# Warm-up of 5 large and 65 small matmuls for 90 small ones, and batch 1's factors split one pair ahead

## The chip, the cores and the metric

The kernel runs on one core of a Trainium2 chip. The core has five engines, each with its own instruction stream: TensorE (PE, matmuls and weight loads), VectorE (DVE), ScalarE (ACT), GpSimd (POOL) and SyncE (SP, which here only issues transfers). The metric is the device time of one execution in microseconds. An engine works its stream in order and waits at an instruction whose semaphores have not arrived. Line numbers (L657) are those of the kernel file.

## What is computed

Chunked attention with a memory, over 4 batches of 768 tokens and 8 heads of 64, and behind it a mixer: a low-rank mixing of tokens and a two-layer network.

```python
for c in range(nc):                       # chunks of 32 queries, 24 of them
    q_c = q[:, :, c_start:c_end]
    k_ctx = k[:, :, l_start:r_end]        # 16 keys to the left, 8 to the right
    k_full = np.concatenate([mem_k, k_ctx], axis=2)
    v_full = np.concatenate([mem_v, v_ctx], axis=2)
    a = softmax(scale * q_c @ k_full.T)   # written out in the reference
    out[:, :, c_start:c_end] = np.matmul(a, v_full)

h = xt @ U @ V                            # xt is x with tokens last
u = x + h.transpose(0, 2, 1)
ch = np.maximum(u @ w_ch1, 0.0) @ w_ch2   # 512 -> 2048 -> 512
return (u + ch).astype(np.float32)
```

The weights U, V, w_ch1 and w_ch2 arrive as 64-bit floating-point words, the rest as 32-bit ones.

## The kernel before

Work goes batch by batch. While the mixer of batch b runs on PE, the attention of batch b + 1 is woven into it, a step at a time. The hidden layer is cut into 16 slices of 128 (f), the 768 tokens into two blocks of 384.

**The front (0 to about 58 us).** Batch 0's attention runs alone. `keep_clock(n, m)` (L144) sets aside n large and m small matmuls on a tile of zeros (`busy`); the next `att_ps` (L135) issues them into the bank that it hands out: large ones 128x512 (L138), small ones 32x64 (L140). Each is a weight load and a matmul, two PE instructions. The first call, `keep_clock(0, START)` (L818) with START = 90 (L30), stands ahead of the first transposes (`turn`, L583).

**Batch 0's mixer (about 57 to 230 us), `both_blocks` (L1187).** For each slice f, `w1_step` (L1119) multiplies by the first weights; ACT makes the rounded hidden values `hh` (L1125), DVE the rest `hl` (L1126); `w2_step` (L1173, L1178) multiplies by the second weights. In the same stage the 64-bit weights are decoded: ACT takes the two halves of the words (L217, L231), DVE joins them (L224, L225, L238), ACT casts the high part (L392, into `w1h`, a `w` pair or `w2last`) and DVE takes the low part (L368). Batch 1's attention is woven in by `place`: key transposes (`turn`, L583, copied by ACT in L601 to L613 into `kall`), query transposes (copied in L643 into `qt`, four copies for a pair of banks), scores (`s_turn`, L657, 128 small matmuls), weights turned (`t_part`, L742), the product with the values (`av_turn`, L760, 128 small matmuls). Transposes, scores and value products of the attention take their banks from one pool of three (`ps_a`), in turn; a bank is free again when what reads it has been read.

**Batches 1 to 3, `fast`.** A pair of slices is worked out with seven products in place of eight (`products`, L1399). The factors of the products are sums of weight blocks, made by GpSimd for batch 1 (`prepare`, L1293) and loaded for batches 2 and 3; `build_factor` splits each into a cast (ACT, L1367, tiles `w1l` for factors 0 to 3 and `s` for 4 to 6) and a rest (DVE, L1368). Some of a pair's factors are split while the pair before it is multiplied. `fold_both` (L1310) turns x of the next batch and forms the folded tokens `th` and `tl`; `put_by` (L1097) notes x tiles for storing, and `let_go` (L1101) issues the stores on ACT (L1104) at the next border.

**What sets the order.** SP's, PE's and GpSimd's streams are in the order of the code. DVE's is so until L1208, ACT's until L1204; from there a scheduler with a simulated timeline orders them by priority. ACT's order in batch 0's mixer (from the third step on) therefore depends on that timeline, the warm-up included, though no code of that stage is touched.

PE's instructions come from memory by a queue of its own (queue 8 in the profile), 16 KB a packet.

Of the kernel before, what the change touches and what calls it, by code (L numbers as in the profile page):

```python
# [26 lines left out]
PACED = {ET.DVE}  # L27
HEAD = {ET.Activation}
FIRST = 3000
START = 90  # L30
FILL = [2, 2, 0, 0, 0, 0]
BANKS = (
    "o0 o1 h h a a a h h a a o0 o1 a a h h o0 o1 a a h h o0 o1 a a o0 o1 a h h a a o0 a a"
# [22 lines left out]
def chunk_attn_then_mixer_kernel(  # L56
# [13 lines left out]
    nc = tc.nc  # L70
# [18 lines left out]
    TB = 3  # L89
# [54 lines left out]
    def keep_clock(n, m=0):  # L144
        warm[0] += n
        small[0] += m
# [23 lines left out]
    for j in range(4):  # L170
        nc.gpsimd.tensor_copy(
            out=rep[32 * j:32 * j + 32],
            in_=ident[32 * j:32 * j + 32, None, 32 * j:32 * j + 32].broadcast_to([32, 3, 32]),
# [252 lines left out]
    def attention(b, xs):  # L426
# [367 lines left out]
        if b == 0:  # L794
# [20 lines left out]
            load_consts()  # L815
            regroup(kraw, kn, "kn", 0)
            regroup(qraw, qn, "qn", 0)
            keep_clock(0, START)  # L818
            k0 = []
            for h in two:  # L820
                k0.append(turn(kn.pop((0, h))))
# [217 lines left out]
    xs = {}  # L1039
# [58 lines left out]
    def put_by(b, t):  # L1098
        held.append((x_d[b, t], xs.pop((b, t))))
# [210 lines left out]
    def fold_both(b):  # L1310
        th, tl = turned[0]
        for tt in range(TB):
            sl = slice(tt * P, (tt + 1) * P)
            with tc.high_priority(offset=HIGH):
                psv = []
                for t in (tt, TB + tt):
                    ps = att_ps()
                    psv.append(ps.rearrange("c (a n) -> c a n", a=NCK))
                    for c in range(NCK):
                        nc.tensor.transpose(out=psv[-1][:, c, :], in_=xs[b, t][:, c * P:(c + 1) * P], identity=ident)  # L1320
                b1, b2 = psv
                f32 = [slot([P, 2, 2, P], F32, "fold") for _ in range(4)]
                base = f32[0]
                nc.scalar.copy(out=base[:, 0], in_=b1[:, 0:2, :])
                nc.scalar.copy(out=base[:, 1], in_=b2[:, 2:4, :])
                for i, ps, c, j, op in (
                    (2, b1, 2, 0, ALU.subtract), (4, b1, 2, 1, ALU.add), (0, b2, 2, 0, ALU.add),
                    (3, b2, 0, 0, ALU.add), (1, b2, 0, 1, ALU.subtract),
                ):
                    nc.vector.tensor_tensor(  # L1330
                        out=f32[1 + i // 2][:, i % 2], in0=ps[:, c:c + 2, :], in1=base[:, j], op=op,
                    )
                for n, (i, m) in enumerate(((5, 2), (0, 2), (2, 2), (4, 1))):
                    nc.scalar.copy(out=th[:, i:i + m, :, sl], in_=f32[n][:, 0:m])
                    nc.vector.tensor_tensor(  # L1335
                        out=tl[:, i:i + m, :, sl], in0=f32[n][:, 0:m], in1=th[:, i:i + m, :, sl].bitcast(F32),
                        op=ALU.subtract,
                    )
            for t in (tt, TB + tt):
                put_by(b, t)  # L1340
            yield

    fast_pools = []
# [15 lines left out]
    factors = {}  # L1359

    def build_factor(p, n):
        if n < WLO:
            s = wlo.tile([P, NCK, P], F32R, name="w1l")
        else:
            s = fast_pools[0].tile([P, NCK, P], F32R, name="s", bufs=len(PRODUCTS) - WLO)
        total = mixed.pop((p, n))
        nc.scalar.copy(out=s[:, 0:2], in_=total)  # L1367
        nc.vector.tensor_tensor(out=s[:, 2:4], in0=total, in1=s[:, 0:2].bitcast(F32), op=ALU.subtract)  # L1368
        factors[p, n] = s
# [10 lines left out]
    def seven(b, kept, last):  # L1380

        th, tl = turned[0]
        ta, tb = fast_pools[1]
        made = {}

        def products(p):
            banks = [ps_h.tile([P, 512], F32, name="ps_h"), ps_a.tile([P, 512], F32, name="ps_a")]
            banks.append(ps_h.tile([P, 512], F32, name="ps_h"))
            banks = [bank_[:, :TOK] for bank_ in banks]
            b1, b2, b3 = banks  # L1390
            kept[2 * p], kept[2 * p + 1] = (
                fast_pools[0].tile([P, TOK], F32, name="kept", bufs=NF // 2) for _ in range(2)
            )
            hid_ = {}
            for n, (i, at_) in enumerate(PRODUCTS):
                s = factors.pop((p, n))
                parts = [(s, c, t, c) for c in range(2) for t in (th, tl)] + [(s, 2 + c, th, c) for c in range(2)]
                for m, (w, wc, t, c) in enumerate(parts):
                    nc.tensor.matmul(  # L1399
                        out=banks[at_], lhsT=w[:, wc, :], rhs=t[:, i, c, :], start=(n < 3 and m == 0),  # L1400
                        stop=(m + 1 == len(parts)), skip_group_check=True,
                    )
                with tc.high_priority(offset=HIGH):
                    if n == 0:
                        nc.scalar.copy(out=ta, in_=b1)  # L1405
                    elif n == 1:
                        nc.vector.tensor_tensor(out=ta, in0=b2, in1=ta, op=ALU.subtract)
                    elif n == 2:
                        nc.vector.tensor_tensor(out=tb, in0=b3, in1=ta, op=ALU.add)  # L1409
                    elif n == 3:  # L1410
                        nc.scalar.copy(out=kept[2 * p], in_=b1)
                    elif n == 4:
                        hid_[1] = split_hidden(b2)
                        nc.vector.tensor_tensor(out=tb, in0=tb, in1=b2, op=ALU.subtract)
                    elif n == 5:
                        nc.vector.tensor_tensor(out=ta, in0=b3, in1=ta, op=ALU.add)  # L1416
                    else:
                        nc.vector.tensor_tensor(out=kept[2 * p + 1], in0=b1, in1=tb, op=ALU.add)
                        hid_[0] = split_hidden(ta)
                    for m in ((5,), (6,), (), (), (), (), ())[n]:  # L1420
                        build_factor(p, m)
                    if p + 1 < NF // 2 or not last:
                        for m in ((), (), (0,), (1, 2), (), (3,), (4,))[n]:
                            build_factor((p + 1) % (NF // 2), m)
                if n in (2, 6):
                    fast_border()
            made[p] = hid_

        def first_block(p):
            hid_ = made.pop(p)  # L1430
            for side in (1, 0):
                f = 2 * p + side
                ends = True if p == NF // 2 - 1 and side == 0 else None
                w2_step(b, 0, f, 0, p == 0 and side == 1, ends, *hid_[side])
                fast_border()

        def second_block(fs, ends, each):
            for f in fs:
                hid_ = split_hidden(kept.pop(f))
                w2_step(b, 1, f, 2, f == fs[0], ends if f == fs[-1] else None, *hid_)  # L1440
                each()

        return products, first_block, second_block
# [90 lines left out]
```

## Time and profile before

| | us |
|---|---|
| median of three runs | 658.36 (656.92 to 664.51) |
| the profiled execution | 658.64 |
| its span, first to last instruction | 656.8 |
| PE busy | 625.0 (95%) |
| DVE busy | 420.6 (64%) |
| ACT busy | 306.1 (47%) |
| GpSimd busy | 77.9 (12%) |

The span is a little shorter than the time, since the time includes what lies around the program. Mean granted PE clock: 0.995 of full speed. A timeline row gives start, duration from the first start to the last end, engine, line, operation, tiles, how many instructions stand in the row and, in brackets, the idle time ahead of it with what ended it; matmuls overlap, so durations of neighbouring rows do too. "issue" means that nothing the profile shows was waited for.

### The profile page before, as it was taken

How to read it: one execution, taken by the hardware profiler on the slowest of the kernel's cores; microseconds unless marked ns; L12 is line 12 of the kernel's file. 1: busy time of each engine (PE TensorE's matmuls, PEld its weight loads, DVE VectorE, ACT ScalarE, POOL GpSimd, SP SyncE). 2: the span in 40 equal slices, each digit the busy share in tenths (PEclk: the TensorE clock that was granted, in tenths of full speed). 3: DMA queues.
4: the chain of work that ended last, by engine and by line, in shares of the span. 5: the costliest groups of instructions: out<-in, count | busy, mean ns of one | idle time of the engine just before them, and what ended most of it. 6: DMA issues, size and time to landing. Idle time of an engine off the chain costs nothing.

```text
span 656.8 us, 15763 instructions
## 1 busy us (share of the span) xinstructions
PE 625.0 (95%) x6196; PEld 547.3 (83%) x6198; DVE 420.6 (64%) x887; ACT 306.1 (47%) x772; POOL 77.9 (12%) x136
## 2 busy tenths in 40 slices
PE   7788999998899898899999999999999999999997
PEld 6567999987778797788788899988979899989986
DVE  4976997886428855556866965645756965427442
ACT  4666676684214445533333646533533643315321
POOL 3700011100021343324400000000000000000000
PEclk9998999999989999999999999999999999999999
DMA  8997684775514659233532489333522673101012
GB/s 208 192 333 255 222 257 156 208 210 143 147 66 160 190 147 241 89 99 130 165 135 83 126 214 222 94 87 112 167 77 83 214 227 97 49 11 38 1 69 76
DMA packets 132724, 95.25 MB, mean 145 GB/s; under 512 B 88746, under 2 KB 109994, under 8 KB 132650
## 3 DMA queue, kind: packets, MB, share of 16 engines
q1 hardware_dynamic: 123130, 72.87, 39.8%
q10 hardware_dynamic: 6480, 11.80, 4.7%
q0 software_dynamic: 3040, 9.57, 3.7%
q8 instruction: 49, 0.80, 0.5%
q14 instruction: 25, 0.20, 0.1%
HBM read 68.65 MB, written 24.64 MB: 142 GB/s over the span
## 4 chain that ended last, share of the span: by engine, by line
PE 79%; DVE 7%; DMA 5%; issue 3%; ACT 3%; SPq 2%; POOL 0%; DVEq 0%; ACTq 0%; POOLq 0%
PE ps_h L1399 18%; PE acc L1173 13%; PE ps_a L1399 7%; PE ps_h L1119 7%; PE acc L1178 6%; PE ps_h L1173 6%; PE ps_a L1173 4%; PE ps_h L1178 3%; PE ps_a L583 2%; PE ps_a L1178 2%; PE ps_a L760 2%; PE ps_a L657 2%; PE ps_h L1165 1%; PE ps_a L742 1%; PE ps_a L1320 1%
## 5 line engine op out<-in xcount | busy, mean ns | idle before, releaser
L1173 PE MATMUL acc<-w,hh 128*128 128x512 f32 x366 | 97.5, 401 | 1.0 <-DVE w L368 1.0
L1399 PE MATMUL ps_h<-th,w1l 128*128 128x384 f32 x288 | 83.4, 343 | 5.1 <-ACT w1l L1367 2.3
L1173 PEld LDWEIGHTS acc<-w,hh 128*128 128x128 f32 x366 | 66.9, 188 | 15.3 <-issue 1.5
L1399 PEld LDWEIGHTS ps_h<-th,w1l 128*128 128x128 f32 x288 | 52.7, 188 | 9.6 <-DVE part L1416 2.9
L1375 DVE SCALAR_TENSOR_TENSOR hl<-kept,hh 128x384 fp32r<-128x384 f32 x48 | 26.7, 557 | 49.0 <-PE ps_a L1178 22.4
L1374 ACT ACTIVATE hh<-kept 128x384 fp32r<-128x384 f32 x48 | 25.4, 530 | 62.2 <-PE ps_a L1173 38.1
L1399 PE MATMUL ps_h<-th,s 128*128 128x384 f32 x192 | 53.0, 337 | 0.2 <-DVE part L1409 0.2
L1178 PE MATMUL acc<-w,hl 128*128 128x512 f32 x183 | 52.3, 394 | 0.0
L1399 PE MATMUL ps_h<-tl,w1l 128*128 128x384 f32 x144 | 48.5, 337 | 0.5 <-DVE tl L1335 0.5
L1173 PE MATMUL ps_h<-w,hh 128*128 128x512 f32 x156 | 43.0, 397 | 0.0
L1119 PE MATMUL ps_h<-uh,w1h 128*128 128x384 f32 x124 | 42.4, 348 | 0.0
L1119 PE MATMUL ps_h<-ul,w1h 128*128 128x384 f32 x124 | 41.2, 340 | 0.0
L1178 PEld LDWEIGHTS acc<-w,hl 128*128 128x128 f32 x183 | 34.8, 190 | 7.6
L1293 POOL TENSOR_TENSOR sums<-val 128x256 f32<-128x256 f32 x40 | 29.9, 762 | 92.3 <-DMA val<-vald 90.0
L1173 PE MATMUL ps_a<-w,hh 128*128 128x512 f32 x132 | 38.3, 394 | 1.7 <-ACT hh L1125 1.7
L1405 ACT COPY part<-ps_h 128x384 f32<-128x384 f32 x24 | 11.5, 480 | 58.8 <-PE ps_h L1399 36.8
L1399 PEld LDWEIGHTS ps_h<-th,s 128*128 128x128 f32 x192 | 35.1, 187 | 0.5 <-issue 0.5
L1367 ACT CAST s<-sums 128x256 fp32r<-128x256 f32 x72 | 28.4, 405 | 14.5 <-PE ps_h L1399 14.4
L1368 DVE TENSOR_TENSOR s<-sums,s 128x256 fp32r<-128x256 f32 x72 | 29.5, 418 | 6.0 <-ACT s L1367 6.0
L1368 DVE TENSOR_TENSOR w1l<-sums,w1l 128x256 fp32r<-128x256 f32 x48 | 24.8, 517 | 13.0 <-ACT w1l L1367 11.7
L1173 PEld LDWEIGHTS ps_h<-w,hh 128*128 128x128 f32 x156 | 28.4, 188 | 5.6
L1125 ACT ACTIVATE hh<-ps_h 128x384 fp32r<-128x384 f32 x31 | 15.1, 490 | 36.9 <-PE ps_h L1119 36.8
(279 smaller groups left out, 1412.5 us busy)
## 6 DMA issues: line engine op xcount, KB each, us to landing
sums<-sumsd SPq DMA_DIRECT2D x32, 256.0 KB
rw<-in_moe_w_ch_dram SPq DMA_DIRECT2D x14, 512.0 KB
xd<-x ACTq DMA_DIRECT2D x27, 256.0 KB
x<-xd SPq DMA_DIRECT2D x27, 256.0 KB
vb<-in_v_dram SPq DMA_DIRECT2D x56, 98.0 KB
raw<-in_moe_w_ch_dram SPq DMA_DIRECT2D x20, 256.0 KB
qn<-in_q_dram SPq DMA_DIRECT2D x36, 128.0 KB
out_dram<-x ACTq DMA_DIRECT2D x18, 256.0 KB
```

Of the source, the lines that this page charges most:

```text
L583: nc.tensor.transpose(out=psv[:, p, r, :], in_=half[:, r, 2 * p:2 * p + 2, :].rearrange("n h d -> n (h d)"), identity=ident,)
L657: nc.tensor.matmul(out=psv[s][CK * i:CK * i + CK, t, p % 2, p // 2, :], lhsT=qt[p // 2][rows, p % 2, NI * t + i, :], rhs=kall[rows, NB * ( ...
L1119: nc.tensor.matmul(out=ph[:, :TOK], lhsT=w[:, c, :], rhs=u[c], start=(m == 0), stop=(m + 1 == len(parts)),)
L1125: nc.scalar.activation(out=hh, in_=ph[:, :TOK], func=AF.Relu)
L1173: nc.tensor.matmul(out=acc[tt], lhsT=h[:, sl], rhs=w, start=(begins and m == 0), stop=False,)
L1178: nc.tensor.matmul(out=acc[tt], lhsT=hl[:, sl], rhs=w2h[f], start=False, stop=ends is not None)
L1293: nc.gpsimd.tensor_tensor(out=two[:, m % 2], in0=a, in1=b_, op=getattr(ALU, op))
L1367: nc.scalar.copy(out=s[:, 0:2], in_=total)
L1368: nc.vector.tensor_tensor(out=s[:, 2:4], in0=total, in1=s[:, 0:2].bitcast(F32), op=ALU.subtract)
L1374: nc.scalar.activation(out=hh, in_=src, func=AF.Relu)
L1375: nc.vector.scalar_tensor_tensor(out=hl, in0=src, scalar=0.0, in1=hh.bitcast(F32), op0=ALU.max, op1=ALU.subtract,)
L1399: nc.tensor.matmul(out=banks[at_], lhsT=w[:, wc, :], rhs=t[:, i, c, :], start=(n < 3 and m == 0), stop=(m + 1 == len(parts)), skip_group_c ...
```

## The change

Three edits. START becomes a pair, 5 large and 65 small matmuls, 140 PE instructions for 180. `fold_both` issues the store of each x tile itself, within the high-priority block, where it had noted it with `put_by`. In `products`, factors 5 and 6 are split in their own pair only where they have not been yet; in batch 1 factors 3 and 4 of the next pair are split after product 5, and 5 and 6 after product 6.

```diff
--- before.py
+++ after.py
@@ -27,7 +27,7 @@
 PACED = {ET.DVE}
 HEAD = {ET.Activation}
 FIRST = 3000
-START = 90
+START = 5, 65
 FILL = [2, 2, 0, 0, 0, 0]
 BANKS = (
     "o0 o1 h h a a a h h a a o0 o1 a a h h o0 o1 a a h h o0 o1 a a o0 o1 a h h a a o0 a a"
@@ -815,7 +815,7 @@
             load_consts()
             regroup(kraw, kn, "kn", 0)
             regroup(qraw, qn, "qn", 0)
-            keep_clock(0, START)
+            keep_clock(*START)
             k0 = []
             for h in two:
                 k0.append(turn(kn.pop((0, h))))
@@ -1336,8 +1336,8 @@
                         out=tl[:, i:i + m, :, sl], in0=f32[n][:, 0:m], in1=th[:, i:i + m, :, sl].bitcast(F32),
                         op=ALU.subtract,
                     )
-            for t in (tt, TB + tt):
-                put_by(b, t)
+                for t in (tt, TB + tt):
+                    nc.scalar.dma_start(out=x_d[b, t], in_=xs.pop((b, t)))
             yield
 
     fast_pools = []
@@ -1417,10 +1417,10 @@
                     else:
                         nc.vector.tensor_tensor(out=kept[2 * p + 1], in0=b1, in1=tb, op=ALU.add)
                         hid_[0] = split_hidden(ta)
-                    for m in ((5,), (6,), (), (), (), (), ())[n]:
-                        build_factor(p, m)
+                    if n < 2 and (p, 5 + n) not in factors:
+                        build_factor(p, 5 + n)
                     if p + 1 < NF // 2 or not last:
-                        for m in ((), (), (0,), (1, 2), (), (3,), (4,))[n]:
+                        for m in (((), (), (0,), (1, 2), (), (3,), (4,)), ((), (), (0,), (1, 2), (), (3, 4), (5, 6)))[b == 1][n]:
                             build_factor((p + 1) % (NF // 2), m)
                 if n in (2, 6):
                     fast_border()
```

In the compiled streams SP's and GpSimd's are unchanged. PE's differs in the warm-up alone. PE, the start of the program (the accumulator bank `acc` and the zero tile `busy`), rows that repeat left out:

```order
-L140 LDWEIGHTS busy
-L140 MATMUL acc_245<-busy 32x64
...
+L138 LDWEIGHTS busy
+L138 MATMUL acc_245<-busy 128x512
...
 L140 LDWEIGHTS busy
 L140 MATMUL acc_245<-busy 32x64
 L583 MATMUL acc_245<-ident,kn 128x128 x4
```

Of the first kind 50 rows go (25 pairs), of the second ten come (5 pairs).

ACT in batch 0's mixer, around 135 us of the trace of before, where batch 1's first queries and second keys are copied out of their banks. Before (`vb` and `dec` are tiles of words under decoding):

```order
L231 ACTIVATE vb_103<-raw 128x256 x2
L392 CAST w2last<-vb_103 128x512
L1125 ACTIVATE hh<-ps_h 128x384
L217 ACTIVATE dec<-rw_1809 128x256
L217 ACTIVATE dec<-raw 128x256
L643 COPY qt<-ps_a 128x2x128 x4
L601 COPY kall<-ps_a 128x2x2x12
L612 COPY kall<-ps_a 128x2x8x16
L613 COPY kall<-ps_a 128x2x7x12
...
L231 ACTIVATE vb_103<-rw_1901 128x256
L231 ACTIVATE vb_103<-raw 128x256
```

The same place of the changed kernel:

```order
L1125 ACTIVATE hh<-ps_h 128x384
L231 ACTIVATE vb_103<-raw 128x256 x2
L392 CAST w2last<-vb_103 128x512
L601 COPY kall<-ps_a 128x2x2x12
L612 COPY kall<-ps_a 128x2x8x16
L613 COPY kall<-ps_a 128x2x7x12
...
L231 ACTIVATE vb_103<-rw_1881 128x256
L231 ACTIVATE vb_103<-raw 128x256
L217 ACTIVATE dec<-rw_1789 128x256
L217 ACTIVATE dec<-raw 128x256
L643 COPY qt<-ps_a 128x2x128 x4
```

hh has moved ahead of the decode of `w2last`, and the copies of the queries (`qt`) from ahead of the key copies to behind them, two more L231 and the two L217 (the three dots stand for a second L612 and L613). Elsewhere between 57 and 147 us ACT's hh and DVE's hl mostly move ahead of a neighbouring decode step.

ACT in batch 1, the first pair of products (`part` and `kept` are sums of products). Before and in the changed kernel alike:

```order
L1367 CAST w1l<-sums 128x256
L1367 CAST w1l<-val 128x256
L1367 CAST w1l<-sums 128x256
L1367 CAST w1l<-val 128x256
...
L1367 CAST s<-sums 128x256 x2
L1411 COPY kept<-ps_h 128x384
L1367 CAST s<-sums 128x256
```

The casts have not moved there, nor have those of the other pairs of batch 1; the stores of x keep their places on ACT, with L1340 for L1104.

## Rows read from the trace of the kernel before

**Rows 1.** The page, part 1 (busy time by engine) and part 3 (PE's instruction queue).

```profile
PE 625.0 (95%) x6196; PEld 547.3 (83%) x6198; DVE 420.6 (64%) x887; ACT 306.1 (47%) x772; POOL 77.9 (12%) x136
...
q8 instruction: 49, 0.80, 0.5%
```

**Rows 2.** Timeline of PE, 152 to 164 us (start, duration, instructions, idle ahead).

```profile
152.63 1.15 PE L657 MATMUL ps_a<-kall,qt 64*32 64x64 f32 x94
155.50 0.54 PE L657 MATMUL ps_a<-kall,qt 64*32 64x64 f32 x34 [1.72 <-issue]
...
158.16 1.04 PE L742 MATMUL ps_a<-ident,pt 128*128 128x128 f32 x8
158.96 1.64 PE L1173 MATMUL acc<-w,hh 128*128 128x512 f32 x6
160.43 0.86 PE L1178 MATMUL acc<-w,hl 128*128 128x512 f32 x3
```

**Rows 3.** Timeline of PE, 176 to 190 us.

```profile
180.61 0.33 PE L760 MATMUL ps_a<-vb,pT 64*32 64x64 f32 x11 [2.59 <-issue]
180.87 1.89 PE L1173 MATMUL acc<-w,hh 128*128 128x512 f32 x6
182.56 1.49 PE L1178 MATMUL acc<-w,hl 128*128 128x512 f32 x3
183.84 1.88 PE L742 MATMUL ps_a<-ident,pt 128*128 128x128 f32 x8
```

**Rows 4.** Transfers, queue 8 in 153.0:153.1, then 177.7:177.8: packets, MB, share.

```profile
q8 instruction: 1, 0.02, 59.5%
...
q8 instruction: 1, 0.02, 94.4%
```

**Rows 5.** Stretches: PE, PEld, DVE, ACT, POOL busy, then granted clock, DMA share, GB/s.

```profile
182.20:185.40 3.20, 3.20 (x13) 2.72 (x12) 0.22 (x1) 0.47 (x1) 0.00 (x0) 0.50 0.02 5
```

**Rows 6.** Timeline of PE, 56 to 63 us.

```profile
58.22 2.06 PE L1173 MATMUL ps_a<-w,hh 128*128 128x512 f32 x6 [1.74 <-ACT hh L1125]
```

**Rows 7.** Timeline of PE, 0 to 10 us.

```profile
1.47 4.22 PE L140 MATMUL acc<-busy 128*32 128x64 bf16 x90 [1.47 <-DVE kall L169]
...
7.31 0.61 PE L288 MATMUL ps_h<-ident,mk 128*128 128x128 f32 x2 [0.60 <-DMA mk<-in_mem_k_dram]
```

**Rows 8.** Timelines of PE (255 to 261 us) and DVE (256 to 260 us).

```profile
258.84 0.42 PE L1399 MATMUL ps_h<-th,w1l 128*128 128x384 f32 x1 [1.45 <-ACT w1l L1367]
...
258.80 0.42 DVE L1368 TENSOR_TENSOR w1l<-sums,w1l 128x256 fp32r<-128x256 f32 x1
```

**Rows 9.** Timeline of PE, 134 to 139.5 us.

```profile
135.58 0.87 PE L1119 MATMUL ps_h<-uh,w1l 128*128 128x384 f32 x4
...
138.23 0.66 PE L583 MATMUL ps_a<-ident,kn 128*128 128x128 f32 x4 [1.34 <-ACT qt L643]
```

**Rows 10.** Timeline of ACT, 134 to 142 us.

```profile
135.31 0.74 ACT L231 ACTIVATE vb<-raw 128x256 int32<-128x256 uint32 x2
135.96 0.60 ACT L392 CAST w2last<-vb 128x512 fp32r<-128x512 f32 x1
136.49 0.49 ACT L1125 ACTIVATE hh<-ps_h 128x384 fp32r<-128x384 f32 x1
136.88 0.43 ACT L217 ACTIVATE dec<-rw 128x256 f32<-128x256 f32 x1
...
137.52 1.23 ACT L643 COPY qt<-ps_a 128x256 f32<-128x256 f32 x4
138.59 0.25 ACT L601 COPY kall<-ps_a 128x48 f32<-128x48 f32 x1
...
139.60 0.52 ACT L231 ACTIVATE vb<-rw 128x256 int32<-128x256 uint32 x1
...
140.25 0.28 ACT L601 COPY kall<-ps_a 128x48 f32<-128x48 f32 x1
```

**Rows 11.** Waits of PE: us in total, times, longest.

```profile
PE ps_h L1399 <- ACT w1l L1367: 2.3, 2, 1.4
```

## The prediction, made before the changed kernel ran

> **What bounds the kernel now.** I read the busy line of the page first: TensorE (PE) is busy 95% of the span, every other engine less than two thirds [rows 1]. So the time is PE's work plus the few microseconds in which PE stands still, and the change leaves PE's work after the warm-up as it is. The question is which stalls go, which come, and what the clock does with them. I then went to PE's timeline for its longest stops, to the DMA queues just ahead of them, and to ScalarE's (ACT's) timeline where the compiled order differs.
>
> Two long stops have "issue" as their end, that is, no semaphore explains them. In the score product of batch 1 (L657), 94 matmuls run, then nothing for 1.72 us, then the other 34 [rows 2]. In a value product (L760) nothing runs for 2.59 us ahead of the last 11 of its 128 [rows 3]. Neither is a place where the program waits. PE's queue for instructions (queue 8) explains them: it moved 49 packets, 0.80 MB, some 16 KB each [rows 1]; PE's 12,394 matmuls and weight loads [rows 1] and some 150 semaphore instructions make 256 for each packet. Such a packet was in flight just ahead of each stop: 59.5% of 16 engines over the 0.1 us from 153.0, and 94.4% over that from 177.7 [rows 4], which are 0.95 and 1.51 us (0.1 x 16 x the share). PE resumed about 1.5 us after they ended (153.0 + 0.95 to 155.50; 177.7 + 1.51 to 180.61). So I take both as waits for a block of instructions that came late.
>
> A stop can cost twice. After the 2.59 us the granted clock stood at 0.50, which is 1.2 GHz, from 182.20 to 185.40 [rows 5]. The same kinds of work at 158 to 161, at full clock, show the price: (1.89 − 1.64) + (1.49 − 0.86) + (1.88 − 1.04) = **1.72 us** [rows 2, 3]. The 1.72 us stop brought no such loss: the rows behind it are those full-clock ones. One at 58 did: 1.74 us idle, and six matmuls that take 2.06 us where 1.64 is the normal [rows 6, 2].
>
> **Edit 1, the warm-up.** Five large pairs and 65 small ones take the place of 90 small pairs. The 25 small pairs that go are 25 x 4.22/90 = 1.2 us [rows 7]; a large one has no row at the slow clock of the start, and by the nearest (six matmuls as wide, half clock, 2.06 us [rows 6]) five take 1.7. The front's first transposes then come about 0.5 us later. The cover: PE waits 0.60 us for the load of mk right behind them [rows 7]. I take 0; without that cover 0.5.
>
> *Block ends.* The 40 instructions that go are 20 matmuls and 20 weight loads, so every later block end falls 20 matmuls on: at L657 from behind matmul 94 to behind 114 of 128; at L760 past the 11 that were left, the six of L1173 and the three of L1178 (11 + 6 + 3 = 20).
>
> At L760 the work ahead of the new end is 0.26 us (180.61 to 180.87), 1.47 (158.96 to 160.43) and 0.86 (the L1178 row): 2.59 us [rows 2, 3]. If the packet starts when it did, nothing of the stop is left. If it starts a fixed time behind the block end before it, it comes later by the time of 20 matmuls there: at 0.10 (L742: 0.80/8) to 0.245 us each (L1173: 1.47/6) 2.0 to 4.9 us, of which I take 2.2 here and 2.7 at L657, since most there are of the short kinds; then 2.2 stay. I take 0.3, nearer the first end, because the packet ran among other transfers. Gain **−2.29**; and with no long stop, the fall of the clock behind it goes too, **−1.72**.
>
> At L657, 20 matmuls are only 20/94 x 1.15 = 0.25 us of work [rows 2]. With the packet at the same moment 1.5 us stay; if PE comes there later against the transfers (below), 0; if the packet moves on by the 2.7, 4.2. I take the middle of the first two, 0.75: **−0.97**.
>
> At 258 a product starts behind 1.45 us of waiting that the view puts down to ACT's cast of its factor, and VectorE (DVE) makes the low half of that factor from 258.80 [rows 8]. A block end lies there too. If it held PE, the gain is bounded by the low half, which ends at 259.22 and is wanted four matmuls on: 0 to −0.4. I take **−0.2**.
>
> *What the order does to ACT.* ACT works its list in order, and the compiled list differs around 135 us. Before, the four copies of the first queries (L643) stand right behind hh (L1125) and two decodes (L217). After, hh stands first, and ahead of the copies come two L231, the cast of L392, five key copies (L601 to L613), two more L231 and the two L217. hh reads the product that PE ends at 136.45 [rows 9], so nothing behind hh runs before its start in the trace, 136.49. From the starts of the ACT rows [rows 10]: hh 0.39, two L231 0.65, L392 0.53, the key copies 138.59 to 139.60 = 1.01, two L231 139.60 to 140.25 = 0.65, two L217 136.88 to 137.52 = 0.64. Then 136.49 + 3.87 = 140.36 is the new start of the query copies; it was 137.52: **+2.84**. PE is who waits: the second key transpose (L583) needs the bank that the first two of the copies empty, and its row says so, 1.34 us idle and ended by ACT's qt [rows 9]. It would start at 138.23 + 2.84 = 141.07, with PE idle for 4.2 us, and batch 0's L1173 queues behind it. Bounds: 0 (if rows that I place behind hh find another gap) and the whole 3.87; I take the value worked out, since ACT has no gap in these rows.
>
> A stop of 4.2 us is longer than those that were followed by the half clock [rows 3, 6], so I add a fall at the price of the other, **+1.72**; bound from below, 0.
>
> **Edits 2 and 3.** In the fold, ACT issues the stores of x directly instead of through a list; in the compiled order they stand at the very same places. The casts of batch 1's factors (L1367) stand in the same order on ACT as before, since the scheduler had already put them there; on DVE a few neighbours swap (L1409, L722, L1368). SyncE and GpSimd show no row of difference. No instruction, transfer or wait is added: 0. What edit 3 could take, if the order hides something, is bounded by the 2.3 us in which PE waited for these casts [rows 11].
>
> **Sum.** +2.84 + 1.72 − 0.97 − 2.29 − 1.72 − 0.2 = **−0.62 us**. The profiled execution took 658.64 us, 0.28 above the median 658.36 of the runs; on the median this gives **657.7**.
>
> **Rivals.**
> - *ACT's new order costs nothing.* Then +2.84 and +1.72 go: 657.7 − 4.56 = 653.1. For it: neighbours move on other engines too, and the list could fit better than old durations say. Against: ACT's rows stand back to back from 135.31 on [rows 10]. Chance 0.20.
> - *The packets start later with the ends* (slower). L657 stops for 4.2 instead of 0.75 (+3.45), L760 for 2.2 instead of 0.3 (+1.9), and the clock falls there as before (+1.72): 657.7 + 7.1 = 664.8. It decides once a packet starts later than the old one by more than the work gained. For it: SyncE's loads, among which the packets run, move with PE. Against: the packets began while many transfers ran [rows 4], which speaks for a delay set by those. Chance 0.15.
> - *The stops are not of blocks, and stay.* Then the gains go and ACT's cost stays: 658.36 + 4.56 = 662.9. Against: both lie between equal matmuls with a packet of instructions ahead. Chance 0.10. The Trainium skill, page "Runtime: NRT & Kernel Launch", section "Instruction fetch mechanics", says that the sequencer fetches the next block while it executes the current one, and that crossing a block's end is mostly hidden; by it the two stops would have another cause and this rival would hold. The trace of before differs at these two places, 1.72 and 2.59 us.
> - *Edit 3 does take PE's waits for the casts.* 657.7 − 2.3 = 655.4 [rows 11]. No row moves, so 0.05.
>
> My forecast holds 0.45; 0.05 is for what I do not see. Its own range is 656.5 to 660: from L657 at 0 (−0.75) and the last bound at 258 (−0.2), to L657 at 1.5, the warm-up's 0.5 and L760 at 1. The wide range, 652.7 to 663.5, takes in all but the slower rival and the unseen. A measurement of this kernel tells about 1% (6.6 us) from nothing. Faster than 651.8 would take the first rival with the fourth or more: 0.06. Slower than 664.9 is nearly half of the slower rival and some of the unseen: 0.09. Within 1%: 0.85.
>
> **What would show it.** Right: L583's wait for ACT's qt near 4.2 us at 137 to 141 and a clock of 0.50 behind it; the L657 run broken at 114, and a shorter stop; no "issue" stop at L760 and no 0.50 at 182. Wrong: L583's wait still near 1.3 (first rival); stops over 2 us behind matmul 114 or the L1178 rows (second); stops still at 94 and 117 (third); L1367's 2.3 us gone (fourth).

## The result: 664.6 us, slower by 0.85%

The changed kernel takes 664.63 us (median of 20 runs, 659.43 to 668.13), the kernel before, run beside it, 658.87 (20 runs, 654.68 to 664.51). The ratio is 1.0085 with a 95% interval of 1.0059 to 1.0111. Forecast were 657.7 and a range of 652.7 to 663.5. The profiled execution took 664.33 us with a span of 662.5, 5.7 over the one before.

The page of the changed kernel, with the lines that answer to [rows 1] and the one of the granted clock:

```profile
PE 627.5 (95%) x6176; PEld 548.0 (83%) x6178; DVE 422.0 (64%) x887; ACT 304.9 (46%) x772; POOL 77.8 (12%) x136
...
PEclk9789999999989999999999999999999999999999
...
q8 instruction: 49, 0.80, 0.5%
```

PE has its 20 matmuls less and works 2.5 us longer; the number of instruction packets is the same. The rest stands still or waits. Where, PE's list of waits says first (us in total, times, longest):

```profile
PE ps_h L657 <- issue: 3.9, 1, 3.9
PE ps_a L657 <- issue: 3.8, 2, 2.5
PE ps_a L760 <- issue: 2.5, 1, 2.5
PE ps_a L583 <- ACT kall L613: 2.3, 1, 2.3
PE acc L760 <- issue: 1.9, 1, 1.9
```

Five "issue" stops of over a microsecond (two stand in the second row), where the kernel before had two. The timeline of PE in the front of the changed kernel (0 to 36 us) has three of them:

```profile
1.48 2.31 PE L138 MATMUL acc<-busy 128*128 128x512 bf16 x5 [1.48 <-DVE kall L169]
3.72 3.24 PE L140 MATMUL acc<-busy 128*32 128x64 bf16 x65
...
9.61 0.39 PE L138 MATMUL ps_h<-busy 128*128 128x512 bf16 x1
10.15 1.44 PE L657 MATMUL ps_h<-kall,qt 64*32 64x64 f32 x123
15.49 0.31 PE L657 MATMUL ps_h<-kall,qt 64*32 64x64 f32 x5 [3.90 <-issue]
...
19.41 1.44 PE L657 MATMUL ps_a<-kall,qt 64*32 64x64 f32 x103 [0.36 <-ACT qt L643]
23.30 0.61 PE L657 MATMUL ps_a<-kall,qt 64*32 64x64 f32 x25 [2.45 <-issue]
...
32.54 0.96 PE L760 MATMUL acc<-vb,pt 64*32 64x64 f32 x65
```

The third splits that value product at 65 of 128 (1.93 us). All three places lie 20 matmuls behind block ends of the kernel before, and those lay inside the same three products, which PE runs through in some 1.5 us. The same places before (timeline of PE):

```profile
9.86 1.48 PE L657 MATMUL ps_h<-kall,qt 64*32 64x64 f32 x128
...
14.97 2.03 PE L657 MATMUL ps_a<-kall,qt 64*32 64x64 f32 x128 [0.32 <-ACT qt L643]
...
29.46 1.40 PE L760 MATMUL acc<-vb,pt 64*32 64x64 f32 x94 [1.50 <-DMA vb<-in_v_dram]
```

Two ends were passed without a stop. The third was no quiet one: 11 matmuls ahead of it PE waited 1.50 us for the values, so that only some 0.4 us of the 1.93 are new. The step that [rows 6] showed at 58.22, the six matmuls behind hh, now starts here:

```profile
64.71 1.64 PE L1173 MATMUL ps_a<-w,hh 128*128 128x512 f32 x6 [1.74 <-ACT hh L1125]
```

That is 6.5 us later than 58.22, and at full clock: the half clock that stood at this place before is gone (1.64 against 2.06, and more behind it). Further on, PE of the changed kernel shows the places of [rows 9, 2, 3] again:

```profile
144.15 0.66 PE L583 MATMUL ps_a<-ident,kn 128*128 128x128 f32 x4 [2.35 <-ACT kall L613]
...
158.55 1.37 PE L657 MATMUL ps_a<-kall,qt 64*32 64x64 f32 x114
161.22 0.34 PE L657 MATMUL ps_a<-kall,qt 64*32 64x64 f32 x14 [1.30 <-issue]
...
186.21 1.09 PE L742 MATMUL ps_a<-ident,pt 128*128 128x128 f32 x8 [0.33 <-issue]
...
189.35 1.28 PE L760 MATMUL ps_a<-vb,pT 64*32 64x64 f32 x105
193.11 0.42 PE L760 MATMUL ps_a<-vb,pT 64*32 64x64 f32 x23 [2.47 <-issue]
```

L583 waits 2.35 us in place of 1.34. L657 stops for 1.30 behind matmul 114 in place of 1.72 behind 94. The stop at L760 is gone but for 0.33 us at L742, which starts 2.4 us later than before (186.21 against 183.84) where the start of this L657 product was 5.9 later (158.55 against 152.63). Then the next value product stops: one block on, its end lies 105 matmuls in. The clock tells the rest (stretches of the changed kernel: busy times of PE, PEld, DVE, ACT, POOL, then granted clock, DMA share, GB/s):

```profile
16.60:20.00 3.40, 3.04 (x54) 2.50 (x59) 2.03 (x6) 2.92 (x11) 1.23 (x2) 0.50 0.99 218
...
23.40:26.80 3.40, 3.40 (x39) 3.23 (x39) 2.79 (x6) 1.22 (x3) 0.03 (x1) 0.50 0.64 132
37.10:40.40 3.30, 3.03 (x16) 1.33 (x14) 3.08 (x11) 2.17 (x6) 1.94 (x5) 0.50 0.63 188
...
194.10:197.40 3.30, 3.30 (x12) 2.08 (x14) 0.92 (x3) 0.00 (x0) 2.73 (x5) 0.50 0.09 35
```

Four stretches at 1.2 GHz, one behind each of the four longest "issue" stops. In the kernel before there were two within the work, at 59 and at 182. The bill of the two profiles, from the starts of like rows: +6.5 by 58 us, −1.6 for the half clock that stood there, +1.0 at L583, −0.4 at L657, about −4 at the old L760 stop with its half clock, about +4 at the new one with its own: 5.5 of the 5.7. Behind 200 us smaller terms of up to 1 us each cancel. This is the bill of one execution of each kernel; other profiles of the same rows start the step behind hh up to 3 us earlier or later (below).

Why do the packets come late in the front? A block is 256 PE instructions. Counted back from matmul 123, the block that ends there is nearly that score product alone (one warm-up matmul of L138 and the 123): PE entered it at 9.4 us and was through at 11.59. Before, the block with its end 20 matmuls earlier begins among the first transposes, and PE was in it from 6.0 to 10.9. The transfers of the changed kernel, 9.4 to 12.9 us, hold no packet of queue 8; it is in flight only in 12.9 to 13.1 (30.1% of 16 engines over 0.2 us, 0.96 us):

```profile
q1 hardware_dynamic: 2463, 1.20, 114.9%
...
q8 instruction: 1, 0.02, 30.1%
```

The loads of the front fill all engines over these 3.5 us. PE ran out of instructions at 11.59, the packet ended near 13.95, and PE went on at 15.49. In the kernel before the first packet was in flight by 6.7 us already (part of queue 8 in 6.0 to 6.7 us), where the engines still had gaps:

```profile
q1 hardware_dynamic: 519, 0.16, 91.2%
q8 instruction: 1, 0.02, 12.0%
```

So two things changed for this block: PE runs through it in 2.0 us where it took 4.9, and its packet, some 6 us later, comes behind the burst of loads.

The Trainium skill, page "Runtime: NRT & Kernel Launch", section "Instruction fetch mechanics", has the crossing of a block mostly hidden. Most of the 49 here are; these are the ones that are not, 0.3 to 4 us each. That it is the blocks shows in the counts: in the 19 profiles of this case, 66 "issue" stops of PE are longer than 0.5 us, and all of them lie at one and the same place of the 256, counted in PE's matmuls and weight loads (to within three, since records can be missing).

### The profile page after: what moved, and what is told of

Its sections match the earlier page's. It is cut to its first block, busy times and chain, and to the rows that moved or that the text cites. A ratio compares the mean times of both kernels' runs of the same rounds, so it can differ in the third digit from the quotient of the medians.

```text
span 662.5 us, 15728 instructions
## 1 busy us (share of the span) xinstructions
PE 627.5 (95%) x6176; PEld 548.0 (83%) x6178; DVE 422.0 (64%) x887; ACT 304.9 (46%) x772; POOL 77.8 (12%) x136
## 4 chain that ended last, share of the span: by engine, by line
PE 85%; DVE 5%; ACT 3%; issue 3%; DMA 2%; POOL 0%; SPq 0%; ACTq 0%; DVEq 0%
PE ps_h L1399 17%; PE acc L1173 14%; PE ps_h L1119 9%; PE ps_a L1399 7%; PE acc L1178 7%; PE ps_h L1173 6%; PE ps_a L1173 5%; PE ps_h L1178 3%; PE ps_a L583 2%; PE ps_a L1178 2%; PE ps_a L657 2%; PE ps_a L760 2%; DMA raw<-in_moe_w_ch_dram 2%; PE ps_h L1165 1%; PE ps_a L1320 1%
## 5 line engine op out<-in xcount | busy, mean ns | idle before, releaser
L1173 PE MATMUL acc<-w,hh 128*128 128x512 f32 x366 | 98.0, 403 | 1.0 <-DVE w L368 1.0
L1173 PEld LDWEIGHTS acc<-w,hh 128*128 128x128 f32 x366 | 67.2, 189 | 15.4 <-issue 1.5
L1178 PE MATMUL acc<-w,hl 128*128 128x512 f32 x183 | 52.4, 395 | 0.0
L1173 PE MATMUL ps_h<-w,hh 128*128 128x512 f32 x156 | 43.0, 397 | 0.0
L1178 PEld LDWEIGHTS acc<-w,hl 128*128 128x128 f32 x183 | 34.8, 190 | 7.6
L1173 PE MATMUL ps_a<-w,hh 128*128 128x512 f32 x132 | 37.8, 390 | 1.7 <-ACT hh L1125 1.7
L1368 DVE TENSOR_TENSOR s<-sums,s 128x256 fp32r<-128x256 f32 x72 | 31.4, 444 | 6.2 <-ACT s L1367 6.2
L1173 PEld LDWEIGHTS ps_h<-w,hh 128*128 128x128 f32 x156 | 28.4, 188 | 5.7
L1399 PE MATMUL ps_h<-tl,s 128*128 128x384 f32 x96 | 32.3, 336 | 0.0
L1407 DVE TENSOR_TENSOR part<-ps_a,part 128x384 f32<-128x384 f32 x24 | 13.3, 555 | 27.5 <-PE ps_a L1399 24.5
```

Source lines behind the costliest of these rows:

```text
L1173: nc.tensor.matmul(out=acc[tt], lhsT=h[:, sl], rhs=w, start=(begins and m == 0), stop=False,)
L1178: nc.tensor.matmul(out=acc[tt], lhsT=hl[:, sl], rhs=w2h[f], start=False, stop=ends is not None)
L1399: nc.tensor.matmul(out=banks[at_], lhsT=w[:, wc, :], rhs=t[:, i, c, :], start=(n < 3 and m == 0), stop=(m + 1 == len(parts)), skip_group_c ...
```

## The experiments

Every comparison has its own runs of the kernel before on the same chip; ratios are to those, with 95% intervals. The same kernel scatters: before's runs lie between 653.7 and 664.5 us, and within one kernel the mean granted clock of a run goes with its time (edits23: 655.6 us at 0.997, 664.0 at 0.989). A single ratio is therefore good for about 0.3%, and conclusions rest on several.

| kernel | PE instructions in the warm-up | large pairs | ACT's order at the query copies | ratio to before |
|---|---|---|---|---|
| edits23 | 180 | 0 | before's | 1.0033 (1.0002 to 1.0064) |
| large10_80 | 180 | 10 | before's | 1.0009 (0.9981 to 1.0037) |
| order_alone | 180 | 2 | changed | 1.0024 (0.9992 to 1.0055) |
| large6_same_count | 180 | 6 | changed | 1.0016 (0.9989 to 1.0042) |
| large_same_count | 180 | 5 | changed | 1.0058 (1.0032 to 1.0084) |
| small_70 | 140 | 0 | before's | 1.0014 (0.9985 to 1.0042) |
| ends_alone | 140 | 3 | before's | 1.0033 (1.0004 to 1.0062) |
| large4_66 | 140 | 4 | before's | 1.0038 (1.0005 to 1.0071) |
| large10_60 | 140 | 10 | changed | 1.0078 (1.0046 to 1.0109) |
| changed_again | 140 | 5 | changed | 1.0071 (1.0041 to 1.0100) |

The column on the order is read from the traces. 180 instructions leave all block ends where they were; 140 move them by 20 matmuls.

**Edits 2 and 3 alone.**

```diff
-START = 5, 65
+START = 0, 90
```

> The warm-up of before (90 small pairs), edits 2 and 3 kept: its compiled rows are those of before on every engine. My theory now (block ends): the loss comes from where PE's instruction blocks end, so this kernel takes 658.9 us within 0.3%, with the stops of before (L657 after 94 matmuls, L760 ahead of the last 11, L583 1.3 us). Rival (edits 2 and 3 cost): a good part of the 5.8 us stays, 661 to 665.

659.36 us against 657.35, ratio 1.0033. The compiled rows are those of before, and so are the stops (L657 again behind 94 matmuls, 1.17 us; L760 again ahead of the last 11, 2.04 us). The 0.3% is what like rows can show here, and its size is the yardstick for the others; beyond it the edits explain nothing. The profiles of like rows scatter as well: here the step behind hh starts at 61.16 us, not at 58.22, and the end that lay in the wait for the values stops PE in its own right (PE, 24 to 32 us):

```profile
30.14 1.35 PE L760 MATMUL acc<-vb,pt 64*32 64x64 f32 x83 [1.46 <-issue]
```

**Large pairs, blocks as before.** `START = 5, 85`, then `START = 6, 84`, then `START = 10, 80`.

> The changed kernel with 5 large and 85 small pairs in the warm-up: 180 PE instructions again, so all blocks end where they did before, but the large pairs and nearly the changed kernel's order on ACT stay. Theory (block ends): no 'issue' stop before 60 us, the stops at L657 (94 of 128) and L760 (ahead of the last 11) back, and of the loss only ACT's order (L583 waits 2.3 us in place of 1.3) and at most 1 us of the longer warm-up: 659 to 661. Rival (the large pairs themselves, by their length or by the clock): 664 or more.

> 6 large and 84 small pairs: 180 PE instructions as before, so blocks end where they did, and the compiled order of every engine is that of before; only the large pairs are new. Theory (large pairs cost by themselves, through a later front): 2 to 4 us over before, 660 to 662. Rival (the 3 to 4 us of the 5-and-85 run were ACT's order and chance): within 1 us of before, L583's wait 1.3 us.

> 10 large and 80 small pairs: 180 PE instructions and the compiled order of before, so only the warm-up is longer, by about 4 us. Theory (a longer warm-up costs little while the blocks end as before; the first packet of instructions is asked for ahead of the front's loads): 0.5 to 2.5 us over before, no 'issue' stop over 1.6 us before 60 us. Rival (the longer warm-up is the loss): 4 us or more.

662.10, 659.02 and 659.23 us. The first came out 1.1 us above its range, with stops of 0.55 and 1.54 us in the front where none was expected. The second lies 1.2 us over before, under its 2 to 4, and was wrong on another point: the trace shows ACT's changed order there too (L583 waits 2.44 us for L613), so only the third has large pairs with before's order. Ten of them (4.45 us, where five take 2.31) cost nothing that can be measured (1.0009), though the front ran later and had two stops over 2 us (2.18 at L657, 2.02 at L760), more than expected. These stops stand at before's own block ends, so an end that is quiet in one front stops PE in a later one. The large pairs by themselves are out as a cause. What the first two have beyond them is ACT's order.

**Ends moved, without the large pairs or with few.** `START = 0, 70`, `START = 4, 66`, `START = 3, 67`.

> 70 small pairs and no large one: 140 PE instructions, so all blocks end as in the changed kernel, with ACT's order close to that of before. Theory (block ends): 'issue' stops in the front at L657 (123 of 128), L657 (103 of 128) and L760 (65 of 128), some 4 to 8 us of them, and 661 to 664.5 in all. Rival (the large pairs): no such stops, 659 or less.

> 4 large and 66 small pairs: 140 PE instructions, blocks end as in the changed kernel, and the compiled order is that of before. Theory (large pairs, block ends and ACT's order add up): about 4 us over before, that is the changed kernel's loss less 1 to 1.5 us, with L583's wait at 1.3 us. Rival (ACT's order is most of the loss): at most 2 us over before.

> 3 large and 67 small pairs: 140 PE instructions, blocks end as in the changed kernel, compiled order that of before on every other engine. Theory (both add up): 1 to 3 us over before, 'issue' stops at L657 (123), L657 (103) and L760 (65) in the front, L583's wait 1.3 us. Rival (the moved ends are the whole loss): 4 us or more over before. Other rival (both needed together): within 0.5 us.

659.52, 660.10 and 661.66 us: 1.0014, 1.0038, 1.0033. The stops of the front are there without a single large pair, at the very places of the changed kernel (timeline of PE, `START = 0, 70`):

```profile
9.68 1.44 PE L657 MATMUL ps_h<-kall,qt 64*32 64x64 f32 x123
13.65 0.31 PE L657 MATMUL ps_h<-kall,qt 64*32 64x64 f32 x5 [2.53 <-issue]
...
20.92 0.43 PE L657 MATMUL ps_a<-kall,qt 64*32 64x64 f32 x25 [2.00 <-issue]
```

So the moved ends make them. But the loss that was expected with them did not come: 659.52 us lies under its 661 to 664.5, 660.10 is 2.3 us over before where about 4 were expected, and only the last is inside its 1 to 3. The three together lie 0.28% over before in the mean, 1.9 us, which is no more than edits23 showed without any move.

**ACT's order alone.** `START = 2, 88`: 180 instructions, and the scheduler happens to give ACT the changed order.

> 2 large and 88 small pairs: 180 PE instructions, blocks end as before, but the scheduler gives ACT the changed kernel's order around the query copies. Theory (moved ends about 2 us and ACT's order about 2 us add up): 1 to 3 us over before, L583's wait 2.3 us on ACT's key copies. Rival (the order costs only the 1.0 us that L583's wait grows): 0 to 1.2 us. Other rival (nearly all of the loss needs both together): within 0.5 us.

660.27 us against 658.72, 1.0024. PE's timeline has the wait at its changed size:

```profile
138.28 0.66 PE L583 MATMUL ps_a<-ident,kn 128*128 128x128 f32 x4 [2.35 <-ACT kall L613]
```

With the two large-pair kernels of that order the mean is 0.33%, 2.2 us, again no more than edits23. The wait itself grows by 1.0; the rest can be the clock, which does not fall behind it every time. It did not in the changed kernel's first profile; it did in its second, 144.7 to 148.0 us:

```profile
144.70:148.00 3.30, 3.30 (x32) 2.17 (x38) 1.81 (x3) 3.30 (x14) 0.00 (x0) 0.50 0.70 224
```

**The changed kernel again, and a longer warm-up with the moved ends** (`START = 10, 60`).

> The changed kernel once more, to stand in one call with the others and to give a second profile. Theory (the loss comes from stops at moved block ends in the front, made longer by the longer warm-up, and from the half clock behind them): again 5 to 6 us over before, with 'issue' stops at L657 (123 of 128), L657 (103) and L760 (65) before 40 us that sum to 7 to 9 us. Rival (its 5.8 us were partly chance of the run): 2 to 4 us.

> 10 large and 60 small pairs: 140 PE instructions, blocks end as in the changed kernel, warm-up longer than there by about 2 us, order on ACT that of the changed kernel. Theory (the first block end comes later the longer the warm-up, and its packet waits behind the loads): at least the changed kernel's loss, 6 to 9 us over before, the first stop at L657 3.5 us or more. Rival (the moved ends cost the same whatever the warm-up): about 2 us plus 1 for the order, 3 us over before.

663.66 and 663.03 us against 658.76: 1.0071 and 1.0078. The loss is there again, 4.9 us, just under the 5 to 6. In the second profile the front's stops are 2.18, 2.59 and 2.35 us, 7.1 in all: their places hold, their lengths change from run to run. The longer warm-up makes nothing worse, so that theory (the first packet comes the later the longer the warm-up) fell.

Do order and ends add up? 0.28% and 0.33% make 0.61%; the result and the two kernels here, with both, have 0.85, 0.71 and 0.78. But the two kernels with neither, edits23 and large10_80, have 0.21% in the mean. Against these, ends alone stand at 0.07%, order alone at 0.12%, both at 0.57%. So the times show a cost of the two together and of neither alone; that they simply add up is not shown, and some 0.4%, 2.5 us, may need both (each of these means is good for about 0.2%).

The profiles hint at the reason. The step behind hh starts at 61.11 and 61.76 us with the ends moved and before's order (`START = 0, 70` and `4, 66`), at 62.62, 63.72 and 64.71 with both, and between 58.22 and 62.11 with the ends of before. The front is thus some 3 us later in the mean where its ends moved (the profiled run of `START = 3, 67`, at 669.2 us, lies 4 us above all its others and is left out). From there to the end of the program the first two take 592.5 and 595.0 us, the three with both 597.8 to 599.2, the six with the ends of before 595.1 to 599.0. So the rest of the program may win back what the front loses as long as ACT keeps before's order. One profile each, with a scatter of up to 3 us, does not prove it.

**Ends moved in other ways.** First in the whole program, by a longer warm-up, `START = 0, 118`:

> 118 small pairs, no large one: 56 PE instructions more than before, so all blocks end 28 matmuls earlier; ACT's order as before. In the run padded by 156 matmuls (28 past a whole block of 128) no 'issue' stop over 0.3 us was left behind 66 us. Theory (block ends): the same here, 4 us gained between 150 and 190 us, and the front as before up to 1 us: 654 to 656 against 658 of before. Rival (the gain was chance or the pad's): L657 and L760 stop again for 1 to 3 us each, 657 to 660.

663.35 us, 1.0082 (1.0047 to 1.0116), the opposite of what was expected: the stops at L657 and L760 did go, but a new one of 4.78 us came in the front, ACT's order was the changed one there as well (L583 2.4 us), and the clock fell behind both. The row, PE of that kernel:

```profile
39.89 0.45 PE L760 MATMUL ps_a<-vbe,pt 64*32 64x64 f32 x11 [4.78 <-issue]
```

Then behind the front only. Small matmuls, whose result is overwritten, go into the bank that L1159 is about to begin, at 56 us, where PE waits for hh anyhow; the front keeps its ends:

```diff
             begins = False
+            if where == 1:
+                for _ in range(PAD):
+                    nc.tensor.matmul(out=acc[0][0:32, 0:64], lhsT=ident.bitcast(BF16)[:, 0:32],
+                                     rhs=ident.bitcast(BF16)[:, 0:64], start=True, stop=True)
             for tt in range(TB):
```

The first of this kind took the identity as fp32, 78 of them:

> Before with 78 small matmuls of the identity added ahead of L1159's second group (at 55.6 us, where PE then waits 1.7 us for hh), so that the front's blocks end as before and all later ones 78 matmuls earlier; the sums are unchanged. Theory (block ends): the front runs as before; the stops at L657 after 94 and at L760 ahead of the last 11 move away from there. Where the later ends miss the dense products, 652 to 656; where they hit others, stops of 2 to 4 us show there and the time is 658 to 664. Rival (the stops belong to the places in the program): both stay at 94 and 117, 658.9 plus up to 0.6.

660.69 us, 1.0041 (1.0019 to 1.0062). In fp32 each ran as two, 156 matmuls in 8.90 us at 57.19, so the ends moved by 156, which is a block's 128 and 28 more. Some 7 us of the padding lie outside the wait, and about 4 of them came back: both old stops were gone, and one of 1.52 us came instead, at 150.80, ahead of the last row of batch 1's first score product. (The expectation of `START = 0, 118` overlooked that one.) Hence the same 28 in bf16, and three other numbers:

> Before with 28 small bf16 matmuls (32x64, on the identity's words) ahead of L1159's second group, inside the 1.7 us in which PE waits there; the front's blocks end as before, the later ones 28 matmuls earlier. ACT's order at the query copies is that of the changed kernel. Theory (block ends): minus 4 us at L657 and L760, plus 1.0 to 1.2 at L583: 654.5 to 656. Rival: the stops stay, 658 to 660.

> Before with 76 small bf16 matmuls (32x64) ahead of L1159's second group, 2.3 us of them against 1.7 us in which PE waits there; the front's blocks end as before, the later ones 76 matmuls earlier, where by the trace of before no block is run through in under 3.6 us (1.6 us in before). ACT's order close to that of before. Theory (block ends): the stops at L657 and L760 go, 4 us, for 0.6 of padding: 653.5 to 655.5. Rival (new stops elsewhere): 657 to 659.

> Before with 20 small bf16 matmuls in PE's wait at 56 us: front as before, later block ends 20 matmuls earlier, ACT's order that of the changed kernel. By the trace of before, the blocks then end nearest to the dense products' ends at 143.5 and 170.1, run through in 2.5 and 2.0 us. Theory (a stop needs a short block, its length set by where the packet falls among other transfers): the stops at L657 (94) and L760 (117) go, one or two of 1 to 3 us show at 145 to 150 and 170 to 178; 656 to 659. Rival (any move of the ends costs): 660 or more.

> The kernel with 20 small matmuls in the wait at 56 us once more, since the same compiled rows have differed by up to 2 us from call to call. Theory (front as before, no late packet behind it): 3 to 5 us under before again, no 'issue' stop over 1.6 us. Rival (chance of the call): within 1.5 us of before.

> 24 in place of 20 small matmuls there: all later blocks end 4 matmuls earlier still; ACT's order is as with 20. Theory (a stop comes only where a block's end lies inside a dense product and its packet is late): as with 20, 654 to 656, unless the first score product, whose end the block's end now nears, stops for up to 1.9 us as with 28. Rival (each place of the ends has its own chance stops): 657 or more.

| small matmuls at 56 us | us | ratio to before |
|---|---|---|
| 20 | 654.68 | 0.9918 (0.9882 to 0.9954) |
| 20, built and run again | 655.80 | 0.9956 (0.9927 to 0.9985) |
| 24 | 655.15 | 0.9952 (0.9923 to 0.9981) |
| 28 | 656.32 | 0.9982 (0.9954 to 1.0010) |
| 76 | 657.13 | 0.9979 (0.9953 to 1.0005) |

With 20 the padding lies inside PE's wait (PE, 54 to 64 us), and batch 1's score and value products run in one piece where they had stopped (PE, 145 to 190 us; line numbers are one or a few higher in this kernel; the rows are of the first of the two):

```profile
55.92 0.76 PE L1160 MATMUL ps_a<-ident 128*32 128x64 bf16 x20
...
58.45 1.66 PE L1177 MATMUL ps_a<-w,hh 128*128 128x512 f32 x6 [0.88 <-ACT hh L1126]
...
153.89 1.48 PE L658 MATMUL ps_a<-kall,qt 64*32 64x64 f32 x128
...
175.97 1.48 PE L761 MATMUL ps_a<-vb,pT 64*32 64x64 f32 x128
```

This is faster than the kernel before, by 2.6 to 4 us, and it pays for ACT's changed order too: its L583 waits 2.35 us. It beat what was expected of 20 (656 to 659): I had expected one or two stops at blocks that are run through in 2.0 and 2.5 us, and none came. Its second build, 2.6 us under before, falls a little short of the 3 to 5 expected; 24 lies inside its range. A short block alone does not make a stop; the packet must also be late: counted out, these two blocks were run through in 2.4 and 1.9 us, but their packets had started 1.3 and 1.9 us before the block ahead of them ended. At L657 and L760 of the kernel before they started 6.0 and 3.1 us after it. With 28 the first score product stopped 1.89 us at the same matmul as with 156, with 76 a value product 2.04 us behind 114, so neither has the whole gain, and both lie above their ranges; the expectation for 76 had counted on long blocks, and one of some 5 us stopped. Moving the ends costs nothing in itself. Where they fall, and when their packets come, decides.

## Why the prediction was wrong

- **"so every later block end falls 20 matmuls on" (edit 1).** This is the step that failed. The working moved all ends, and then asked what that does at L657, at L760 and at 258, and nowhere else. The other 46 of the 49 were put at nothing without a word. Three of them stop PE in batch 0's score and value products, for 3.90, 2.45 and 1.93 us with half-clock stretches behind them (some 0.4 of the last is new), and one in a later value product (2.47 us). Before's own timeline would have shown that the first of these blocks shrinks from 4.9 us to 2.0. How these stops and ACT's order share the loss stays open: the times show it for the two together alone.
- **The warm-up's length (0).** It was rightly held to be small: five large pairs took 2.31 us where 1.7 was taken, and the first transposes came 1.3 us later and not 0.5, but the wait for mk covered most of it (the first score product starts at 10.15 against 9.86), and ten large pairs gave 1.0009.
- **The gain at L760 (−2.29, −1.72).** Right at its place: 0.33 us left (0.3 was taken) and full clock at 182. But it was given back at 193 by the next value product and the half clock behind it.
- **L657 (−0.97).** The place was right, behind 114; 1.30 us stayed where 0.75 was taken. Other profiles of these ends have between none and 1.05.
- **ACT's order (+2.84, +1.72).** The wait was found where it was said to be, but sized wrongly: 2.35 us, +1.0. The step that failed is the bank. The working kept the second key transpose on the bank that the query copies empty. In the changed kernel the row names L613, the key copies: with ACT's order the bank it gets had changed too, to that of the first key transpose. The copies that it waits for end 2.6 us into the list of 3.87 that I had added up, and the query copies come behind them. The fall of the clock behind it came in one of two profiles of the changed kernel. This term was too high, so it hid part of what edit 1 lacked.
- **258 (−0.2).** The block end is gone from there, and the product waits 0.69 and 0.22 us where it had waited 1.45: −0.5.
- **Edits 2 and 3, 0.** Held.
- **Rivals.** The measured time is within 0.3 us of the slower rival's 664.8, but not by its mechanism: its stops behind matmul 114 and the L1178 rows were to be 4.2 and 2.2 us, and were 1.30 and 0.33. So the near hit is luck. Only its condition, a packet that starts later than the old one by more than the work gained, was the one that mattered, and it held in the front, where I had not looked (12.9 us against 6.7). The rival with blocks out of play is refuted: the stops went or moved with the ends in every kernel that moved them.
- **The range** took its bounds from terms at three block ends and ACT's order; a move that reaches all 49 ends needed a term for the ones that were quiet. One profile was also read as if it were the kernel: where a stop's length and the clock's falls are partly chance, each term has a spread of 1 to 2 us of its own.

## What to carry to other kernels

When an edit adds or removes instructions, every later block end moves: place each of them, not only those that stopped before, and look for blocks that the engine now runs through quickly while the transfers ahead are dense. A few harmless instructions inside a wait move the ends behind them alone, which is a tuning knob of its own (here 0.4 to 0.8% with 20 or 24, less with 28 or 76). And when a scheduler's order changes, buffers may be dealt out anew: ask again which buffer a wait is for. Two changes that cost nothing measurable one by one can cost something together, so compare with kernels that have neither as well as with the kernel before.

## What the runs showed of the hardware

- A block of 256 PE instructions that came late stopped PE for up to 4.8 us here, and PE went on 1.2 to 1.7 us after the packet's end in all 66 stops over 0.5 us (about 1.5 at 155.50 and 180.61 before and at 15.49 after).
- Of like idle stretches some are followed by the half clock and some are not: 2.35 us at L583 was in the second profile of the changed kernel, not in the first; 1.74 us ahead of L1173 was before, not after. In one set of runs before's 35 lie between 654.4 and 662.1 us, with mean granted clocks of 0.989 to 1.0.
- The kernel with 20 small matmuls, which has no "issue" stop behind its front, scatters less than before: seven runs lay within 653.5 to 654.9 us, where before's beside them run from 653.7 to 664.3, and twelve later ones within 652.6 to 658.3, against 654.0 to 664.3. That the stops make the scatter is not shown.
